# A linear-attention and token-MLP kernel: a fixed order of work, mix in token order, and stores of whole tiles

## The chip, the cores and the metric

The kernel runs on one core of one Trainium2 chip. The metric is the device time of one execution in microseconds (us), as the median of several executions. A profile is one execution; its span is about 2 us shorter than its time.

PE is TensorE's matmul side and PEld its weight loads. DVE is VectorE, ACT is ScalarE, POOL is GpSimd, and SP issues transfers. A copy or activation that brings a product from PSUM to SBUF is called an eviction.

## The reference

There are 8 batches, 8 heads, 576 tokens and 64 elements per head, in fp32. This is the reference without its set-up:

```
q_p = concat(relu(q) * cos, relu(q) * sin)       # cos and sin of the token's position
k_p = concat(relu(k) * cos, relu(k) * sin)
kv  = einsum('bhsf,bhsd->bhfd', k_p, v);  z = sum of k_p over tokens
x   = (q_p kv) / (q_p z + 1e-6)                  # then heads joined: 8 x 576 x 512
wq, wk = x @ w_q, x @ w_k                        # 512 -> 64
W      = wq wk^T / 8                             # token by token, per batch
mixed  = W x
out    = relu(mixed) @ w_out                     # 8 x 576 x 512
```

The kernel never makes W: it forms wk'x (64 x 512), then mixed = wq (wk'x).

## The kernel before

A load of one head puts nine successive tokens of that head in one partition: partition d (0 to 63 for one head, 64 to 127 for the next) holds tokens 9d to 9d+8. The kernel calls the place within the nine "c". One load brings four heads, and the table numbers these groups from 0 to 15 ("heads" in some of the texts below). Everything after that runs in **slot order**, c*64 + d, while the output in memory is in **token order**, 9*d + c. The kernel before keeps slot order to the end and lets its stores do the change, with 64 rows each:

```
    def mx(b, st, eng):                      # mixed, transposed: two 128 x 288 halves
        ...
        for r in range(2):
            nc.tensor.matmul(mx_ps[:, r, 0:hs],
                kxs[b][64 * r:64 * r + 64, dmc * P:(dmc + 1) * P],
                wqTs[b][64 * r:64 * r + 64, nh, :], start=True, stop=True)
        c0 = (b % 2) * S + nh * hs
        dst = mix_sb.rearrange("p (r i) n -> p r i n", r=2)[:, :, i, c0:c0 + hs]
        nc.scalar.activation(dst, mx_ps[:, :, 0:hs], AF.Relu, scale=scale_moe)   # dense in and out
        ...

    def wout(bp, rt0, n, engs):              # output tiles of 128 slots
        ...
                nc.tensor.matmul(o_ps[:, r, :], mixs[bp][:, dmc, rt * P:(rt + 1) * P],
                    wo_sb[:, dmc, :], start=(dmc == 0), stop=(dmc == NDM - 1))
        ...
            for hi in range(2):              # two stores of 64 rows, every 9th row of the output
                bloc, j0 = divmod(P * (rt0 + r) + 64 * hi, S)
                dst = dataclasses.replace(
                    out, offset=out.offset + (2 * bp + bloc) * S * DM + (j0 // 64) * DM,
                    ap=[[C9 * DM, 64], [1, DM]])
                nc.sync.dma_start(dst, o_sb[hi * 64:hi * 64 + 64, r, :])
```

The other parts that change: x is transposed by 10 matmuls of 128 rows per half batch. wq and wk are separate products, wk with 20 matmuls of 64 columns per batch. wk'x is 5 matmuls of 512 columns. All products of the token MLP share two PSUM buffers. The order comes from one loop over pairs of heads that mixes in the MLP of earlier batches.

Of the kernel before, what the change touches and what calls it, by code (L numbers as in the profile page):

```python
# [16 lines left out]
I32 = mybir.dt.int32  # L17
AF = mybir.ActivationFunctionType
ALU = mybir.AluOpType
FMAX = 3.4028234e38  # L20
EPS_HI = 9.9837780e-07


@with_exitstack
def kernel(
# [21 lines left out]

    NB = 2 * B
# [4 lines left out]
    inp = ctx.enter_context(tc.tile_pool(name="inp", bufs=4))  # L53
    prep = ctx.enter_context(tc.tile_pool(name="prep", bufs=2))
    small = ctx.enter_context(tc.tile_pool(name="small", bufs=3))
    xpool = ctx.enter_context(tc.tile_pool(name="xpool", bufs=3))
    moe = ctx.enter_context(tc.tile_pool(name="moe", bufs=2))
    mixpool = ctx.enter_context(tc.tile_pool(name="mixpool", bufs=2))
    outpool = ctx.enter_context(tc.tile_pool(name="outpool", bufs=3))
# [3 lines left out]
    def m2_tile(dtype, name):  # L63
        return psum.tile([P, 2, 512 if dtype is FP32 else 1024], dtype,
                         name=name, tag="m2", bufs=2)

    srcs = {}
    for nm, src in (("k", k), ("q", q), ("v", v)):
        srcs[nm] = [src[b].flatten().rearrange("(pr p e) -> p pr e", pr=NPAIR, p=P)
                    for b in range(B)]  # L70
    raw = {}

    def load(H, nsplit=1, names=("k", "q", "v")):
        b, h0 = divmod(2 * H, NPAIR)
        step = 2 // nsplit
        for nm in names:
            raw[nm, H] = inp.tile([P, 2, HC], FP32, name=f"{nm}f")
        for sp in range(nsplit):
            for nm in names:
                lo = sp * step  # L80
                nc.sync.dma_start(raw[nm, H][:, lo:lo + step, :],
                                  srcs[nm][b][:, h0 + lo:h0 + lo + step, :])

    load(0, nsplit=2)

    warm = consts.tile([P, 512], BF16)
    nc.vector.memset(warm, 1.0)
    warm_ps = m2_tile(FP32, "warm_ps")

    def warm_up(n):  # L90
        for _ in range(n):
            nc.tensor.matmul(warm_ps[:, 0, :], warm[:, 0:P], warm,
                             start=True, stop=True)

    warm_up(14)

    wq_f = consts.tile([P, NDM, DH], FP32)
    wk_f = consts.tile([P, NDM, DH], FP32)
    wo_f = consts.tile([P, NDM, DM], FP32)

    coef = math.pi / 2.0 / S
    ki = consts.tile([P, C9, 2], I32)
    qi = consts.tile([P, C9, D], I32)
    for hh in range(2):
        ph = slice(64 * hh, 64 * hh + 64)
        nc.gpsimd.iota(ki[ph, :, 0], pattern=[[-1, C9]], base=S, channel_multiplier=-C9)
        nc.gpsimd.iota(ki[ph, :, 1], pattern=[[1, C9]], base=0, channel_multiplier=C9)
    nc.gpsimd.iota(qi[0:64], pattern=[[-1, C9], [-C9, D]], base=S, channel_multiplier=0)
    nc.gpsimd.iota(qi[64:128], pattern=[[1, C9], [C9, D]], base=0, channel_multiplier=0)
    cossin = consts.tile([P, C9, 2, D], BF16)  # L110
    cst = consts.tile([P, C9, D], BF16)
    nc.scalar.activation(cossin, ki.unsqueeze(3).to_broadcast([P, C9, 2, D]),
                         AF.Sin, bias=0.0, scale=coef)
    nc.scalar.activation(cst, qi, AF.Sin, bias=0.0, scale=coef)

    ident = consts.tile([P, P], BF16)
    make_identity(nc, ident)

    ones_t = consts.tile([P, P], BF16)
    nc.gpsimd.memset(ones_t, 1.0)  # L120
    eps_t = consts.tile([P, SC], BF16)
    nc.gpsimd.memset(eps_t, 0.0)
    nc.gpsimd.memset(eps_t[0:1, :], EPS_HI)
    nc.gpsimd.memset(eps_t[32:33, :], 1.0e-6 - EPS_HI)

    v_bufs, qpt_bufs, xT_bufs = [], [], []
    for i in range(3):
        vb = consts.tile([P, 2, C9, D + 2], BF16, name=f"v_buf{i}")
        nc.gpsimd.memset(vb[:, :, :, D:D + 2], 1.0)
        v_bufs.append(vb)  # L130
    for i in range(3):
        qb = consts.tile([P, 2, SLOTS, D], BF16, name=f"qpt_buf{i}")
        nc.gpsimd.memset(qb[:, :, 0, :], 0.0)
        qpt_bufs.append(qb)
    for i in range(2):
        xb = consts.tile([P, NDM, SLOTS * D], BF16, name=f"xT_buf{i}")
        nc.gpsimd.memset(xb[:, :, 0:D], 0.0)
        xT_bufs.append(xb)

    wqq_sb = consts.tile([P, NDM, 2, DH], BF16)  # L140
    wk_sb = consts.tile([P, NDM, DH], BF16)
    wo_sb = consts.tile([P, NDM, DM], BF16)

    def load_w():
        nc.sync.dma_start(wq_f, moe_w_q.rearrange("(c p) j -> p c j", p=P))
        nc.sync.dma_start(wk_f, moe_w_k.rearrange("(c p) j -> p c j", p=P))
        nc.sync.dma_start(wo_f, moe_w_out.rearrange("(c p) n -> p c n", p=P))

    def cast_w(part):
        if part == 0:  # L150
            nc.scalar.copy(wqq_sb, wq_f.unsqueeze(2).to_broadcast([P, NDM, 2, DH]))
            nc.scalar.copy(wk_sb, wk_f)
        else:
            nc.scalar.copy(wo_sb[:, 2 * part - 2:2 * part, :],
                           wo_f[:, 2 * part - 2:2 * part, :])

    kp, qd, rks = {}, {}, {}

    def relu_k(H, lo, hi, eng):
        if lo == 0:  # L160
            rks[H] = prep.tile([P, 2, C9, D], BF16, name="rk")
        o = rks[H][:, lo:hi].rearrange("p r c d -> p r (c d)")
        if eng is nc.scalar:
            nc.scalar.activation(o, raw["k", H][:, lo:hi, :], AF.Relu)  # L164
        else:
            eng.tensor_scalar(o, raw["k", H][:, lo:hi, :], FMAX, 0.0,
                              op0=ALU.min, op1=ALU.max)

    def mul_k(H, lo, hi):
        if lo == 0:  # L170
            kp[H] = prep.tile([P, 2, C9, 2, D], BF16, name="kp")
        n = hi - lo
        nc.vector.tensor_mul(  # L173
            kp[H][:, lo:hi],
            rks[H][:, lo:hi].unsqueeze(3).to_broadcast([P, n, C9, 2, D]),
            cossin.unsqueeze(1).to_broadcast([P, n, C9, 2, D]))

    def cast_v(H, lo, hi, eng):
        src = raw["v", H][:, lo:hi, :].rearrange("p r (c d) -> p r c d", c=C9)
        dst = v_bufs[H % 3][:, lo:hi, :, 0:D]  # L180
        if eng is nc.scalar:
            nc.scalar.copy(dst, src)
        else:
            eng.tensor_scalar(dst, src, 1.0, 1.0, op0=ALU.mult, op1=ALU.mult)  # L184

    def dup_q(H, lo, hi, eng):
        if lo == 0:
            qd[H] = prep.tile([P, 2, C9, 2, D], BF16, name="qd")
        n = hi - lo
        dst = qd[H][:, lo:hi].rearrange("p r c w d -> p (r c) w d")  # L190
        src = raw["q", H][:, lo:hi, :].rearrange(
            "p r (c d) -> p (r c) d", c=C9).unsqueeze(2).to_broadcast(
                [P, n * C9, 2, D])
        if eng is nc.scalar:
            nc.scalar.activation(dst, src, AF.Relu)
        else:
            eng.tensor_scalar(dst, src, FMAX, 0.0, op0=ALU.min, op1=ALU.max)  # L197

    xs, kvs, xTs, wkjs, wqTs, kxs, mixs = {}, {}, {}, {}, {}, {}, {}

    def qk_pe(g):
        H, i = divmod(g, 2)
        qk_ps = psum.tile([P, 2, 2048], mybir.dt.uint8, name="qk_ps", bufs=1)
        qt = qk_ps[:, :, 0:2 * HC].bitcast(BF16)
        kvp = qk_ps[:, :, 2 * HC:2 * HC + 4 * (D + 1)].bitcast(FP32)
        for c in range(C9):
            for hh in range(2):
                p0 = hh * 64
                nc.tensor.matmul(  # L209
                    kvp[:, hh, :], kp[H][p0:p0 + 64, i, c, :, :],  # L210
                    v_bufs[H % 3][p0:p0 + 64, i, c, 0:D + 1],
                    start=(c == 0), stop=(c == C9 - 1))
        for c in range(C9):
            for hh in range(2):
                p0 = hh * 64
                nc.tensor.transpose(  # L216
                    qt[:, hh, c * D:(c + 1) * D],
                    qd[H][p0:p0 + 64, i, c, :, :],
                    ident[p0:p0 + 64, p0:p0 + 64])
        kv_sb = small.tile([P, 2, D + 1], BF16, name="kv_sb")  # L220
        nc.vector.tensor_copy(kv_sb, kvp)  # L221
        kvs[g] = kv_sb
        nc.vector.tensor_mul(  # L223
            qpt_bufs[g % 3][:, :, 1:SLOTS, :],
            qt.rearrange("f h (c d) -> f h c d", c=C9),
            cst.unsqueeze(1).to_broadcast([P, 2, C9, D]))
# [226 lines left out]
```

## Time and profile before

| | before |
|---|---|
| time, median of 3 | 151.56 us (150.58 to 152.74) |
| span of the profile | 149.6 us |
| PE, DVE, ACT, POOL busy | 115.7, 90.6, 88.1, 56.8 us |
| granted TensorE clock | mostly about half from 10 to 30 us, nearly always full after that |

The prediction shows the rows of busy time and of transfers. Three more lines are needed later. The first two are from the groups of instructions: line, engine, operation, output and input, shapes, count, then busy time in us and mean ns of one, then the idle time before them and what ended it. The third is the main transfer queue: packets, MB, and its share of 16 engines' span.

```profile
L316 ACT ACTIVATE mix_sb<-mx_ps 128x576 bf16<-128x576 f32 x29 | 17.5, 655 | 4.7 <-PE mx_ps L309 4.7
L309 PE MATMUL mx_ps<-wqT,kx 64*128 64x288 bf16 x64 | 8.0, 285 | 7.0 <-ACT xT_buf L260 3.9
...
q1 hardware_dynamic: 20448, 39.07, 81.2%
```

The mix evictions are a small group, 17.5 us of ACT at **655 ns** each. The queue's share is 81.2% of 149.6 = 122 us.

### The profile page before, as it was taken

What the parts mean: (1) busy time and instruction counts of PE and PEld (TensorE: products, weight loads), DVE (VectorE), ACT (ScalarE), POOL (GpSimd) and SP (SyncE); (2) the same over time, 40 slices, a digit from 0 to 9 for tenths busy, and PEclk for the clock granted to TensorE, in tenths of its full rate; (3) what the DMA queues carried; (4) which work ended last, traced back from release to release, by engine and by line L of the source; (5) the groups of instructions that cost most, each with busy time, mean ns of one, the idle gap of its engine ahead of it and who ended that gap; (6) DMA issues with size and microseconds to landing.
All of it is one profiled execution on the core that took longest, in us unless ns stands there. A gap on an engine that the chain in (4) does not pass through costs nothing. (4 is left out here: it accounts for less than half of the span.)

```text
span 149.6 us, 4978 instructions
## 1 busy us (share of the span) xinstructions
PE 115.7 (77%) x2155; PEld 77.5 (52%) x2182; DVE 90.6 (61%) x156; ACT 88.1 (59%) x114; POOL 56.8 (38%) x56
## 2 busy tenths in 40 slices
PE   6924663969889988998898987888989896894910
PEld 2214553856567657654765665557656664461400
DVE  1278363979777685947596957375959563325110
ACT  8230076467977787668768757687784566243220
POOL 7638248683561808160817164408170000000000
PEclk9985576589999999999999999999999999999996
DMA  5999999999988999996999998999921811566195
GB/s 163 307 397 338 390 391 391 391 390 390 391 279 182 332 302 323 328 379 148 296 326 343 318 400 278 314 296 307 329 81 42 184 31 24 116 143 142 24 203 124
DMA packets 20469, 39.38 MB, mean 263 GB/s; under 512 B 3040, under 2 KB 3040, under 8 KB 20448
## 3 DMA queue, kind: packets, MB, share of 16 engines
q1 hardware_dynamic: 20448, 39.07, 81.2%
q8 instruction: 17, 0.28, 0.7%
q14 instruction: 4, 0.03, 0.1%
HBM read 29.62 MB, written 9.44 MB: 261 GB/s over the span
## 5 line engine op out<-in xcount | busy, mean ns | idle before, releaser
L197 POOL TENSOR_SCALAR qd<-qf 128x2304 bf16<-128x2304 f32 (+1 forms) x17 | 35.6, 2092 | 52.1 <-PE qk_ps L216 30.6
L327 PE MATMUL o_ps<-wo_sb,mix_sb 128*128 128x512 bf16 x124 | 33.6, 379 | 3.6 <-ACT mix_sb L316 1.8
L164 ACT ACTIVATE rk<-kf 128x1152 bf16<-128x1152 f32 (+1 forms) x17 | 18.9, 1111 | 18.4 <-DMA kf<-in_k_dram 9.2
L260 ACT COPY o_sb<-o_ps 128x512 f32<-128x512 f32 (+1 forms) x24 | 18.4, 765 | 17.9 <-PE o_ps L327 8.3
L242 DVE TENSOR_TENSOR x_sb<-num_ps,rec 128x640 bf16<-128x640 f32 x32 | 26.4, 825 | 1.1
L221 DVE CAST kv_sb<-qk_ps 128x130 bf16<-128x130 f32 x32 | 9.4, 293 | 26.7 <-PE qk_ps L216 26.4
L209 PE MATMUL qk_ps<-v_buf,kp 64*128 64x65 bf16 x576 | 15.8, 199 | 11.0 <-POOL v_buf L184 7.2
L223 DVE TENSOR_TENSOR qpt_buf<-qk_ps,cst 128x1152 bf16<-128x1152 bf16 x32 | 23.9, 748 | 0.0
L173 DVE TENSOR_TENSOR kp<-rk,cossin 128x2304 bf16<-128x2304 bf16 (+1 forms) x17 | 22.2, 1305 | 1.6 <-ACT rk L164 1.6
L327 PEld LDWEIGHTS <-mix_sb 128*128 128x128 bf16 x144 | 13.3, 97 | 15.2 <-issue 3.1
L209 PEld LDWEIGHTS <-kp 64*128 64x128 bf16 x576 | 11.9, 99 | 17.2 <-issue 8.7
L316 ACT ACTIVATE mix_sb<-mx_ps 128x576 bf16<-128x576 f32 x29 | 17.5, 655 | 4.7 <-PE mx_ps L309 4.7
L260 ACT COPY xT_buf<-xT_ps 128x1152 bf16<-128x1152 bf16 x15 | 16.8, 1119 | 4.8 <-PE xT_ps L252 4.8
L184 POOL TENSOR_SCALAR v_buf<-vf 128x1152 bf16<-128x1152 f32 x15 | 17.3, 1151 | 1.2
L236 PE MATMUL num_ps<-kv_sb,qpt_buf 128*128 128x65 bf16 x320 | 17.4, 202 | 0.0
L236 PEld LDWEIGHTS <-qpt_buf 128*128 128x128 bf16 x320 | 13.4, 102 | 3.6 <-issue 1.7
L216 PE MATMUL qk_ps<-ident,qd 64*128 64x64 bf16 x576 | 14.8, 197 | 0.0
L309 PE MATMUL mx_ps<-wqT,kx 64*128 64x288 bf16 x64 | 8.0, 285 | 7.0 <-ACT xT_buf L260 3.9
L252 PE MATMUL xT_ps<-ident,x_sb 128*128 128x128 bf16 x160 | 12.2, 227 | 0.2 <-ACT mix_sb L316 0.2
L216 PEld LDWEIGHTS <-qd 64*128 64x128 bf16 x576 | 11.8, 100 | 0.0
L252 PEld LDWEIGHTS <-x_sb 128*128 128x128 bf16 x160 | 10.4, 102 | 1.9 <-issue 0.2
L239 PE MATMUL num_ps<-eps_t,ones_t 128*128 128x5 bf16 x64 | 11.2, 174 | 0.0
(44 smaller groups left out, 97.9 us busy)
## 6 DMA issues: line engine op xcount, KB each, us to landing
out_dram<-o_sb SPq DMA_DIRECT2D x72, 128.0 KB, 3.3
kf<-in_k_dram SPq DMA_DIRECT2D x15, 576.0 KB, 6.7
qf<-in_q_dram SPq DMA_DIRECT2D x15, 576.0 KB, 7.7
vf<-in_v_dram SPq DMA_DIRECT2D x15, 576.0 KB, 8.5
wo_f<-in_moe_w_out_dram SPq DMA_DIRECT2D x1, 1024.0 KB, 9.9
kf<-in_k_dram SPq DMA_DIRECT2D x2, 288.0 KB, 4.0
qf<-in_q_dram SPq DMA_DIRECT2D x2, 288.0 KB, 4.3
vf<-in_v_dram SPq DMA_DIRECT2D x2, 288.0 KB, 5.3
```

The lines of the kernel that those rows point to most:

```text
L164: nc.scalar.activation(o, raw["k", H][:, lo:hi, :], AF.Relu)
L173: nc.vector.tensor_mul(kp[H][:, lo:hi], rks[H][:, lo:hi].unsqueeze(3).to_broadcast([P, n, C9, 2, D]), cossin.unsqueeze(1).to_broadcast([P, ...
L197: eng.tensor_scalar(dst, src, FMAX, 0.0, op0=ALU.min, op1=ALU.max)
L209: nc.tensor.matmul(kvp[:, hh, :], kp[H][p0:p0 + 64, i, c, :, :], v_bufs[H % 3][p0:p0 + 64, i, c, 0:D + 1], start=(c == 0), stop=(c == C9 - 1))
L216: nc.tensor.transpose(qt[:, hh, c * D:(c + 1) * D], qd[H][p0:p0 + 64, i, c, :, :], ident[p0:p0 + 64, p0:p0 + 64])
L223: nc.vector.tensor_mul(qpt_bufs[g % 3][:, :, 1:SLOTS, :], qt.rearrange("f h (c d) -> f h c d", c=C9), cst.unsqueeze(1).to_broadcast([P, 2, ...
L236: nc.tensor.matmul(nv[:, hh, u, :], qpt_bufs[g % 3][:, hh, 2 * u:2 * u + 2, :], kvs[g][:, hh, :], start=(u == 0), stop=False)
L242: nc.vector.tensor_tensor(xs[b][:, :, 2 * pr:2 * pr + 2, :].rearrange("p u h d -> p h u d"), nv[:, :, :, 0:D], rec.to_broadcast([P, 2, SC, ...
L252: nc.tensor.transpose(xT_ps[:, i, u * P:(u + 1) * P], xs[b][:, u, 2 * hp:2 * hp + 2, :], ident)
L260: nc.scalar.copy(dst, src)
L316: nc.scalar.activation(dst, mx_ps[:, :, 0:hs], AF.Relu, scale=scale_moe)
L327: nc.tensor.matmul(o_ps[:, r, :], mixs[bp][:, dmc, rt * P:(rt + 1) * P], wo_sb[:, dmc, :], start=(dmc == 0), stop=(dmc == NDM - 1))
```

## The change

The intent is to drop the loop's order for a table that places each piece of work, on its engine and in its PSUM bank, and to save work on the way. TensorE gets cheaper transposes, wq and wk come from one product, and wk'x runs in pairs of 64-column tiles. Mix is written in token order, so a store is 128 partitions with whole rows next to each other. The core of the diff:

```diff
-    inp = ctx.enter_context(tc.tile_pool(name="inp", bufs=4))
+N_RAW, N_RK, N_KP, N_QD, N_VB, N_QPT, N_KV = 5, 2, 3, 3, 3, 4, 4
+N_XS, N_XT, N_WQK, N_WKJ, N_KX, N_MIX, N_OSB = 3, 2, 2, 2, 2, 2, 5
+ORDER = """
+LD.k.0.0@Y LD.k.0.1@Y LD.q.1.0@Y LD.k.1.0@Y LD.v.1.0@Y LD.q.0.1@Y LD.v.0.1@Y LD.q.0.0@Y
+... (55 lines in all: piece @ engine and, for TensorE, PSUM bank)
+"""
+    banks = psum.tile([P, 8, 2048], U8, name="banks")
 ...
-                nc.tensor.transpose(xT_ps[:, i, u * P:(u + 1) * P],
-                    xs[b][:, u, 2 * hp:2 * hp + 2, :], ident)
+                for r in range(2):
+                    p0 = 64 * r
+                    T.transpose(xv[:, r, i, u, :],
+                                xs[b % N_XS][p0:p0 + 64, u, 2 * hp:2 * hp + 2, :],
+                                ident[p0:p0 + 64, p0:p0 + 64])
 ...
-                nc.tensor.matmul(wk_ps[:, 0, u * DH:(u + 1) * DH], ...)       # 20 per batch
+                T.matmul(w[:, nh, :], wqk_sb[:, dmc, :], ...)                  # wq and wk at once
+            T.transpose(t[:, u * DH:(u + 1) * DH], wqk[b % N_WQK][64:128, u * P:(u + 1) * P], ...)
 ...
-            nc.tensor.matmul(kx_ps[:, 0, :], wkjs[b][:, u, :, :], xs[b][:, u, :, :], ...)
+            for r in range(2):
+                T.matmul(o[64 * r:64 * r + 64, :], wkj[b % N_WKJ][:, u, :],
+                         xs[b % N_XS][:, u, 4 * r:4 * r + 4, :], ...)
 ...
-        dst = mix_sb.rearrange("p (r i) n -> p r i n", r=2)[:, :, i, c0:c0 + hs]
+        c0, c1 = ((0, 5), (5, 9))[nh]
+        src = bank2(at["MX", b, j], 0, 4 * n, FP32).rearrange(
+            "p r (c d) -> p r c d", d=D)
+        dst = mix[b // 2 % N_MIX].rearrange("p (r i) n -> p r i n", r=2)[
+            :, :, i, o:o + S].rearrange("p r (d c) -> p r c d", c=C9)[:, :, c0:c1, :]
 ...
+            cols = mix[b // 2 % N_MIX][:, dmc, base:base + step * P].rearrange(
+                "p (n s) -> p s n", s=step)[:, r, :]
 ...
-                nc.sync.dma_start(dst, o_sb[hi * 64:hi * 64 + 64, r, :])
+        eng.dma_start(out_rows[r0:r0 + step * P, :].rearrange("(p s) n -> p (s n)", s=step),
+            osb[n % N_OSB][:, 0:step, :].rearrange("p s n -> p (s n)"))
```

## The prediction

> **What bounds the kernel now.** I read the page first, then busy time by stretches, then the waits, then the timeline of one steady period. From the page (part 1's PE row; then granted clock, DMA share and GB/s over 40 slices of 3.74 us):
>
> ```profile
> PE 115.7 (77%) x2155; PEld 77.5 (52%) x2182; DVE 90.6 (61%) x156; ACT 88.1 (59%) x114; POOL 56.8 (38%) x56
> ...
> PEclk9985576589999999999999999999999999999996
> DMA  5999999999988999996999998999921811566195
> GB/s 163 307 397 338 390 391 391 391 390 390 391 279 182 332 302 323 328 379 148 296 326 343 318 400 278 314 296 307 329 81 42 184 31 24 116 143 142 24 203 124
> ```
>
> No engine is full over the span. The first 42 us run at 390 GB/s: there loads are the limit, and TensorE, short of work, falls to half clock (10 to 30 us). After that come stretches, in which one holds neither loads nor full engines:
>
> ```profile
> 60.00:80.00 20.00, 18.13 (x340) 11.92 (x345) 15.01 (x26) 14.06 (x19) 8.54 (x5) 1.00 0.92 299
> ...
> 110.00:120.00 10.00, 9.07 (x202) 6.23 (x203) 6.77 (x13) 6.01 (x9) 1.15 (x1) 1.00 0.48 106
> 120.00:130.00 10.00, 8.14 (x110) 5.12 (x110) 4.40 (x9) 5.72 (x8) 0.00 (x0) 1.00 0.25 56
> 130.00:140.00 10.00, 7.52 (x57) 4.01 (x59) 3.49 (x5) 3.33 (x7) 0.00 (x0) 1.00 0.48 107
> ```
>
> Columns: stretch, length, busy PE, PEld, DVE, ACT, POOL, granted clock, DMA share, GB/s. From 60 to 80 us PE is 91% busy and DMA 92%. In the last three rows there are hardly any loads: DMA at share 0.48 moves 106 GB/s, that is 106/0.48 = 221 GB/s per full share, where the loads made 390 at a share of about 1.06 (the stretches of 10 to 30 us), 369. So **a stored byte costs DMA 1.7 times a loaded one**. 29.62/0.369 + 9.44/0.221 = 80 + 43 = 123 us of DMA share, and 81.9% of 149.6 us is 122.5: it adds up.
>
> The steady period (one batch) is 62.00 to 77.10 us on the timeline, 15.1 us. Its pieces, by start to start (a PE end is modelled, so busy time overstates):
>
> ```profile
> 68.92 0.82 DVE L242 TENSOR_TENSOR x_sb<-num_ps,rec 128x640 bf16<-128x640 f32 x1
> 69.66 1.35 DVE L173 TENSOR_TENSOR kp<-rk,cossin 128x2304 bf16<-128x2304 bf16 x1
> ...
> 71.06 0.30 DVE L221 CAST kv_sb<-qk_ps 128x130 bf16<-128x130 f32 x1
> 71.27 0.75 DVE L223 TENSOR_TENSOR qpt_buf<-qk_ps,cst 128x1152 bf16<-128x1152 bf16 x1
> 71.33 0.72 PE L252 MATMUL xT_ps<-ident,x_sb 128*128 128x128 bf16 x10
> 73.25 0.74 PE L268 MATMUL wk_ps<-wk_sb,xT_buf 128*128 128x64 bf16 x20 [0.34 <-ACT xT_buf L260]
> 74.95 1.24 PE L293 MATMUL kx_ps<-x_sb,wkj 128*128 128x512 bf16 x4
> ```
>
> PE per batch: 4 k/v and q-transpose blocks of 0.65 (2.6), 4 numerators of 0.35 (1.4), 2 xT of 0.55 (1.1), wk 0.67, wk'x 1.08, wq 1.07, mix 0.72, 4.5 output tiles of 0.86 (3.9): 12.5 us, so 2.6 of 15.1 are waits. DVE per pair of heads: 0.21 + 0.67 + 0.25 + 0.74 + half of 1.40 = 2.57, four make 10.3 us. DMA per batch: 3.54 MB at 390 plus 1.18 MB at 221 x 1.06 = 9.1 + 5.0 = 14.1 us. **The steady part is thus bound by PE's order and its waits, with DMA only 1.0 us behind**; from 110 us on it is a serial tail. The waits say the same, the others wait for PE:
>
> ```profile
> POOL qd L197 <- PE qk_ps L216: 30.6, 8, 5.8
> DVE kv_sb L221 <- PE qk_ps L216: 26.4, 16, 2.6
> ```
>
> **What the Trainium skill says.** "SBUF — State Buffer", section "Door 1: The DMA port swizzle": partitions 0..63 reach 8 of 16 ports, with an asymptote of half the rate. The 64-row stores here at 221 against 369 agree in direction; the 128-row ones should then cost what loads cost. The same page, "Who interferes with whom": a DVE instruction with two SBUF inputs and a GpSimd one that reads SBUF exclude each other, the second waits. The trace agrees: these two rows are 0.43 and 0.85 us longer than their usual 1.35 and 2.11, and each began while the other engine's was running.
>
> ```profile
> 28.09 1.78 DVE L173 TENSOR_TENSOR kp<-rk,cossin 128x2304 bf16<-128x2304 bf16 x1
> 11.83 2.96 POOL L197 TENSOR_SCALAR qd<-qf 128x2304 bf16<-128x2304 f32 x1 [2.58 <-DMA qf<-in_q_dram]
> ```
>
> "TensorEngine Tiling (Array Packing)", "Tiling Modes": 64-row and 64-column tiles run in parallel, but a change of mode drains. For rows the trace agrees (18 of the 64-row matmuls start within 0.29 us, 16 ns each, where 64 columns at full clock alone would be 29 by the page "TensorE: Matmul & The Clock Gate", "Back-to-back issue gap": N/2.4 + 2.5); for column tiles no run here shows it yet.
>
> **The change part by part** (counts from the table of the changed kernel, durations from above).
> *PE.* xT becomes 20 transposes of 64 rows: 20 x 16 ns = 0.32 for 0.55, twice, -0.46. The 20 wk matmuls go (-0.67), 5 small transposes come (+0.13). wk'x is 10 matmuls of 256 columns in pairs: 0.54 for 1.08 if the pair runs together, no gain if not. Sum: 12.5 - 1.5 = 11.0 us per batch.
> *DMA.* Stores of 128 rows and 4 KB: if they cost what loads do, 39.07 MB/390 = 100 us in all for 116 at before's rates, 12.1 us per batch. Input rings go from 4 to 5 deep and stores are placed where their data is ready, so SP should not block loads. All inputs and the stores ahead of the last load are 33 MB: that load lands at 33/0.39 + 2.5 = 87 us at best.
> *ACT and POOL.* ACT gives 9 of the k relus to POOL and some evictions to DVE and takes 8 v casts: about 78 us. POOL about 59 + 4. Neither binds.
> *DVE.* The base stays 32 x 2.57 = 82 us. From ACT it gets 7 output evictions, 4 xT, 4 mix, 4 smaller, one copy and one relu: 21 pieces of about 0.65 less 0.08 overlap, 13 to 14 us. Sum **96 us: DVE becomes the fullest engine**, 11 to 14 us in each batch's part of the table (PE 8 to 12, DMA 11 to 13 there).
>
> *The path.* (a) Start: head pairs 3 and 2 come first. Their loads are 2.36 MB; in the kernel before that many bytes had landed at about 10.3 us; a v cast of 1.16 follows; first matmul at 11.5 to 12, with DVE having done 2.7 us of its 96. (b) From there to the last wq/wk product, DVE has 88.8 us in the table. If it were never idle the middle would take 88.8. I add two terms: collisions with POOL, which is busy over half of this time now while before it mostly started behind PE (3 collisions in 15): 16 products x 0.3 us = 5 us; and 6% idle from an order that waits for evictions and, at the start, from a half-clock PE: (88.8 + 5)/0.94 = 99.8. Here the 6% is my choice. (c) Tail from the last wq/wk product: PE has 11.9 us in the table; the chain of product, eviction, transpose, eviction, wk'x, eviction, mix, two evictions, five output tiles, eviction is about 11.5 to 12.2. Then a store: about 3 us where before needed 6.4 after its last eviction (143.15 to 149.6) as stores were queued. 15.3. Sum 12 + 99.8 + 15.3 = 127.1 for the span; time was span + 2.0 before: **129**; with no collisions and no idle it would be 118. I put the point between, nearer the first, as a fixed table is likely to have been fitted to such durations: **127.5**.
>
> **Rivals.** (1) *DMA takes over*: if mixed stores still cost 221, the stores before the last load add 3.4 MB x (1/0.234 - 1/0.39) = 6 us, last load at 93; behind it about 5 us to the last x, still not later than DVE (12 + 88.8). It would cost 0 to 4 us. For it: shares of 0.92 already now. Against: the port argument. (2) *Fixed order, PE stalls*: PE is in order too; wherever the table's guess of a landing time is wrong, every engine waits in turn. Eight PSUM banks instead of a fixed pair per use speak against; the idle would then be 12 to 15%, and the time 134 to 138. (3) *POOL and DVE lock each other* more: all 16 products wait 0.85 us (a mean rest of a POOL piece), 13 us instead of 5: 136. (4) *Nothing is gained since DMA was near its bound anyway*: against it is the 42 us tail after 107 us with DMA at 0.2 to 0.5, of which the change takes about half by starting the later batches' work earlier.
>
> **Range and chances.** Low: 118 plus a little, 120. High: rivals 2 or 3 at full size, 136. Faster by over 2% needs less than 148.5, which takes 20 us of idle on top: 0.96. Same 0.025, slower 0.015.
>
> **What would show it.** Right: DVE busy near 100 us and over 75% of the span; the k product's mean above 1.4 us; first k/v matmul near 12 us; stores alone at over 300 GB/s per share; loads finished before 95 us; wk'x half as long start to start; under 4 us from last eviction to end. Wrong: a largest wait of DVE on PE still over 20 us; a DMA share of 0.95 or more up to the last load with DVE waiting for inputs; strided output weights making the output tile slower than 0.86 us; PE at half clock beyond 35 us.

## The result

The changed kernel takes **185.49 us** (median of 4, 184.87 to 187.64), and the kernel before 151.07 in the same rounds. Ratios here are the mean time of one kernel's fast runs over that of the other's of the same rounds, so not quite the ratio of the medians. This one is 1.235, with a 95% interval of 1.224 to 1.246. The change made the kernel 23% slower, where the prediction said 127.5 and gave "slower" a chance of 0.015.

The page of the changed kernel: busy time by engine, then granted clock, DMA share and GB/s over 40 slices of 4.65 us, the main transfer queue, and the chain of work that ended last, by engine and by line.

```profile
PE 130.0 (70%) x2262; PEld 82.6 (44%) x2262; DVE 105.1 (57%) x177; ACT 132.6 (71%) x111; POOL 66.5 (36%) x60
...
PEclk9955855996579579965859786995598559985599
DMA  5999999999993086028999918100052022021245
GB/s 167 326 402 392 378 361 390 388 390 390 391 389 131 0 261 240 4 99 304 374 350 379 301 49 303 60 4 0 0 231 111 28 90 99 18 113 56 113 174 221
...
q1 hardware_dynamic: 17904, 39.06, 57.7%
...
PE 40%; ACT 33%; issue 11%; DVE 8%; DMA 5%; SPq 1%; ACTq 0%; DVEq 0%
ACT mix L385 29%; PE banks L402 13%; PE banks L243 6%; PE banks L275 6%; DMA vf<-in_v_dram 5%; PE banks L252 5%; PE banks L326 3%; DVE mix L387 3%; PE banks L371 3%; PE banks L354 2%; DVE kp L215 2%; PE banks L309 2%; DVE qpt L262 2%; ACT xT L170 1%; SPq L191 1%
```

ACT has gone from 88.1 to 132.6 us and is now the engine with the largest share. The granted clock falls to half again and again in the whole span: its mean is 0.761, where it is 0.925 in experiment 1, which has the same table and short evictions. The queue's share did what was hoped: 57.7% of 185.9 = 107 us, where it had 122. The groups say where ACT's time went:

```profile
L385 ACT ACTIVATE mix<-banks 128x640 bf16<-128x640 f32 (+1 forms) x28 | 75.0, 2811 | 8.7 <-PE banks L371 8.7
...
L371 PE MATMUL banks<-wqk,kx 64*128 64x320 bf16 (+1 forms) x32 | 10.3, 345 | 12.7 <-ACT mix L385 12.6
...
L387 DVE TENSOR_SCALAR mix<-banks 128x640 bf16<-128x640 f32 (+1 forms) x4 | 10.7, 2769 | 3.7 <-PE banks L371 3.7
```

One mix eviction costs **2811 ns where it cost 655**, on DVE 2769. They move as much as before: 640 and 512 elements by turns, for 576. So 28 of them fill 75.0 us of ACT. The last line of the page's chain has these evictions as 29% of the span on ACT and 3% on DVE, so they are on the path, and a piece of the timeline shows how (start, length, engine, what; in brackets the idle time before and what ended it):

```profile
57.32 3.35 ACT L385 ACTIVATE mix<-banks 128x640 bf16<-128x640 f32 x1
60.72 0.42 PE L371 MATMUL banks<-wqk,kx 64*128 64x320 bf16 x1 [3.84 <-ACT mix L385]
61.20 3.01 ACT L385 ACTIVATE mix<-banks 128x640 bf16<-128x640 f32 x1 [0.54 <-PE banks L371]
62.71 0.29 DVE L172 CAST kvs<-banks 128x130 bf16<-128x130 f32 x1 [4.02 <-PE banks L252]
64.26 0.68 PE L243 MATMUL banks<-vb,kp 64*128 64x65 bf16 x18 [1.59 <-ACT mix L385]
```

PE waits 3.84 us for an eviction to give back its banks. DVE waits 4.02 us for PE. Then the next eviction holds PE again.

### The profile page after: what moved, and what is told of

The parts are those of the page before. It is cut to its first block, busy times and chain, and to the rows that moved or that the text cites. A ratio compares the mean times of both kernels' runs of the same rounds, so it can differ in the third digit from the quotient of the medians.

```text
span 185.9 us, 5159 instructions
## 1 busy us (share of the span) xinstructions
PE 130.0 (70%) x2262; PEld 82.6 (44%) x2262; DVE 105.1 (57%) x177; ACT 132.6 (71%) x111; POOL 66.5 (36%) x60
## 3 DMA queue, kind: packets, MB, share of 16 engines
q1 hardware_dynamic: 17904, 39.06, 57.7%
## 4 chain that ended last, share of the span: by engine, by line
PE 40%; ACT 33%; issue 11%; DVE 8%; DMA 5%; SPq 1%; ACTq 0%; DVEq 0%
ACT mix L385 29%; PE banks L402 13%; PE banks L243 6%; PE banks L275 6%; DMA vf<-in_v_dram 5%; PE banks L252 5%; PE banks L326 3%; DVE mix L387 3%; PE banks L371 3%; PE banks L354 2%; DVE kp L215 2%; PE banks L309 2%; DVE qpt L262 2%; ACT xT L170 1%; SPq L191 1%
## 5 line engine op out<-in xcount | busy, mean ns | idle before, releaser
L385 ACT ACTIVATE mix<-banks 128x640 bf16<-128x640 f32 (+1 forms) x28 | 75.0, 2811 | 8.7 <-PE banks L371 8.7
L402 PE MATMUL banks<-wo_sb,mix 128*128 128x512 bf16 x144 | 45.3, 458 | 5.2 <-ACT mix L385 3.8
L262 DVE TENSOR_TENSOR qpt<-banks,cst 128x1152 bf16<-128x1152 bf16 x32 | 23.6, 749 | 16.9 <-PE banks L252 13.6
L243 PE MATMUL banks<-vb,kp 64*128 64x65 bf16 x576 | 18.9, 217 | 16.6 <-ACT mix L385 6.9
L275 PE MATMUL banks<-kvs,qpt 128*128 128x65 bf16 x320 | 18.7, 216 | 10.7 <-ACT mix L385 8.9
L292 DVE TENSOR_TENSOR xs<-banks,rec 128x640 bf16<-128x640 f32 x32 | 25.3, 807 | 0.2
L275 PEld LDWEIGHTS <-qpt 128*128 128x128 bf16 x320 | 17.3, 113 | 16.6 <-issue 12.8
L170 ACT COPY osb<-banks 128x512 f32<-128x512 f32 x29 | 19.2, 674 | 6.7 <-PE banks L402 6.6
L170 ACT COPY xT<-banks 128x1280 bf16<-128x1280 bf16 x12 | 15.2, 1263 | 6.1 <-PE banks L309 6.0
L180 POOL TENSOR_SCALAR rk<-kf 128x1152 bf16<-128x1152 f32 (+1 forms) x11 | 12.9, 1170 | 16.7 <-DVE kp L215 15.3
L252 PE MATMUL banks<-ident,qd 64*128 64x64 bf16 x576 | 18.2, 215 | 0.0
L387 DVE TENSOR_SCALAR mix<-banks 128x640 bf16<-128x640 f32 (+1 forms) x4 | 10.7, 2769 | 3.7 <-PE banks L371 3.7
```

What stands on the lines that cost most here:

```text
L170: A.copy(dst, src)
L180: eng.tensor_scalar(dst, src, FMAX, 0.0, op0=ALU.min, op1=ALU.max)
L243: T.matmul(kvp[:, hh, :], kp[H % N_KP][p0:p0 + 64, i, c, :, :], vb[H % N_VB][p0:p0 + 64, i, c, 0:D + 1], start=(c == 0), stop=(c == C9 - 1))
L252: T.transpose(qt[:, hh, c * D:(c + 1) * D], src, ident[p0:p0 + 64, p0:p0 + 64])
L262: eng.tensor_mul(qpt[g % N_QPT][:, :, 1:SLOTS, :], qk_views(at["QK", g])[0].rearrange("f h (c d) -> f h c d", c=C9), cst.unsqueeze(1).to_b ...
L275: T.matmul(nv[:, hh, u, :], qpt[g % N_QPT][:, hh, 2 * u:2 * u + 2, :], kvs[g % N_KV][:, hh, :], start=(u == 0), stop=(u == SC - 1 and not ...
```

## The experiments

The first question was what makes the eviction slow. The changed write is the suspect: its last dimension steps through mix by 9 elements, 18 bytes, where before it was dense. Rival A: it is the eviction's other new features (larger pieces, reading from banks shared by all). Rival B: the table itself starves the kernel, and slow evictions only show it. The second question, once that was known, was why the mended kernel is still 10 us above the prediction.

### 1. Only the write made dense (a wrong result)

```diff
-            :, :, i, o:o + S].rearrange("p r (d c) -> p r c d", c=C9)[:, :, c0:c1, :]
+            :, :, i, o:o + S].rearrange("p r (c d) -> p r c d", c=C9)[:, :, c0:c1, :]
```

The rows then come out in slot order (relative error 0.498), and all else is as in the changed kernel.

> The changed kernel with one edit: the mix evictions write side by side in slot order instead of every 18 bytes, so output rows are in the wrong places on purpose; table, counts and sizes are as they were. Theory A (the stride of 18 bytes makes each of the 32 mix evictions 2.8 us in place of about 0.7): evictions 0.6 to 0.75 us, ACT busy falls from 132.6 by 28 x 2.1 = 59 to about 74 us, time 120 to 135 us. Rival B (the fixed order itself stalls, and the long evictions are a symptom of waiting on something): evictions stay above 2 us or the time stays above 165 us.

Measured: 137.85 us (137.08 to 139.06), ratio to before 0.914 (0.905 to 0.924). The same groups, with the shapes kept apart:

```profile
L385 ACT ACTIVATE mix<-banks 128x640 bf16<-128x640 f32 x14 | 9.9, 706 | 12.0 <-PE banks L371 8.5 <-PE banks L402 3.5
L385 ACT ACTIVATE mix<-banks 128x512 bf16<-128x512 f32 x14 | 8.2, 597 | 8.8 <-PE banks L371 4.5 <-PE banks L402 4.3
```

This one line of addressing is worth 47.6 us. ACT's evictions lost 75.0 - 18.1 = 56.9 us and DVE's 10.7 - 3.0 = 7.7. The time gained is three quarters of that. PE's busy time fell too, from 130.0 to 105.8 us, as the clock stayed up. Rivals A and B fall: size, banks and table are unchanged. The same table also gives a kernel faster than the one before.

### 2. Token order read from PSUM (correct)

The change of order moves to the other side. The product covers 32 of the 64 partitions' tokens, so that one eviction holds 288 whole successive tokens. The eviction reads PSUM with a step and writes densely.

```diff
-            w = (wqk[...][0:64, D + c0 * D:D + c1 * D] if r == 0
-                 else wq2[...][64:128, c0 * D:c1 * D])
+            w = (wqk[...][0:64, D:D + S] if r == 0 else wq2[...][64:128, :]).rearrange(
+                     "p (c d) -> p c d", c=C9)[:, :, d0:d1]     # d0, d1 = 0, 32 or 32, 64
 ...
-            "p r (c d) -> p r c d", d=D)
+            "p r (c d) -> p r d c", c=C9)                        # source: step of 32 in PSUM
-            :, :, i, o:o + S].rearrange("p r (d c) -> p r c d", c=C9)[:, :, c0:c1, :]
+            :, :, i, o:o + n].rearrange("p r (d c) -> p r d c", c=C9)   # dense
```

> Token order kept and result right: mix products are cut by the 32-token halves instead of by slots, so an eviction reads PSUM with a stride of 128 bytes and writes 288 neighbours densely. Theory A1 (only strided writes into SBUF are slow): evictions about 0.7 us, time as e1. Theory A2 (strided reads of PSUM cost the same): evictions 2.3 to 3 us, time 180 to 190 us.

Measured: **137.91 us** (137.42 to 139.6), ratio 0.911 (0.900 to 0.922), correct.

```profile
L385 ACT ACTIVATE mix<-banks 128x576 bf16<-128x576 f32 x28 | 17.9, 652 | 20.0 <-PE banks L372 12.2 <-PE banks L402 7.7
```

An eviction that reads PSUM with a step of 128 bytes costs 652 ns, as much as the dense one of the kernel before. So token order itself costs nothing; the side on which it is made decides.

### 3. Token order read by TensorE (correct)

Here the matmul's moving operand is read in token order, and the eviction is dense on both sides.

```diff
-            ... else wq2[...][64:128, c0 * D:c1 * D])
+            ... else wq2[...][64:128, :]).rearrange("p (c d) -> p d c", c=C9)[:, d0:d1, :]
```

> Token order kept and result right: the permutation is done by TensorE, whose moving operand of the mix product is read with a stride of 128 bytes; evictions are dense on both sides. Theory A with a free strided moving read: time as e1 (120 to 135 us). If the moving read is slowed by 4 like the writes, the 64 mix matmuls go from about 125 to 500 ns, pairs side by side, 12 us more TensorE work: 125 to 147 us. Rival B: above 165 us.

Measured: 141.25 us (140.29 to 142.2), ratio 0.936 (0.926 to 0.946).

```profile
L372 PE MATMUL banks<-wqk,kx 64*128 64x288 bf16 x32 | 19.6, 644 | 1.8 <-ACT mix L384 1.7
...
127.59 0.66 PE L372 MATMUL banks<-wqk,kx 64*128 64x288 bf16 x1
128.07 0.66 PE L372 MATMUL banks<-wqk,kx 64*128 64x288 bf16 x1
```

One mix product takes 644 ns where it takes 296 in experiment 2, and the kernel is 3.3 us slower than experiment 2 (141.25 against a mean of 137.95 of the fast runs). The mean of one hides the true price, because successive products overlap. Start to start, two of them lie 0.48 us apart in the two lines of the timeline above, and 0.12 us in experiment 2 (125.88 and 126.00 us), both at full granted clock. So TensorE pays for the step too, by about the same factor of four as ACT, on less work: 32 pairs times 0.36 us are 11.5 us (an estimate from these starts), of which 3.3 reached the time.

### 4. The stepped write put into the kernel before (a wrong result)

```diff
-        dst = mix_sb.rearrange("p (r i) n -> p r i n", r=2)[:, :, i, c0:c0 + hs]
+        dst = mix_sb.rearrange("p (r i) n -> p r i n", r=2)[:, :, i, c0:c0 + hs].rearrange(
+            "p r (d c) -> p r c d", c=C9)            # every 9th place of the half's 288
+        src = mx_ps[:, :, 0:hs].rearrange("p r (c d) -> p r c d", c=C9)
-            nc.scalar.activation(dst, mx_ps[:, :, 0:hs], AF.Relu, scale=scale_moe)
+            nc.scalar.activation(dst, src, AF.Relu, scale=scale_moe)
```

> The kernel before with only the write of its mix evictions changed to a step of 9 elements (rows wrong on purpose). Theory A: 29 evictions on ACT and 3 on DVE go from 0.66 to about 2.6 us, ACT busy from 88 to about 145 us, time 180 to 205 us. Rival B (the write is harmless, the table is the cause): 150 to 156 us.

Measured: 206.49 us (203.37 to 210.49). Two of its four runs, the profiled one among them, were slow, so the 2867 ns below come from a slow run; the two fast ones took 205.85 and 203.37, ratio 1.356 (1.334 to 1.378).

```profile
L318 ACT ACTIVATE mix_sb<-mx_ps 128x576 bf16<-128x576 f32 x29 | 76.6, 2867 | 5.5 <-PE mx_ps L309 5.5
```

The write alone brings the evictions of the kernel before to 2867 ns, as in the changed one, and costs it 53 us. With experiment 1 this is the cause from both ends: taken away, it gives 47.6 us back; put in, it takes 53.

### 5. The cost of a step, measured by itself

Experiment 2 was followed, after its last product, by copies of 256 elements per partition with various steps, three of each (one look; 198.45 us with these copies).

```diff
+    for _ in range(3):
+        A.copy(flatA[:, 0:256*s].rearrange("p (n s) -> p n s", s=s)[:, :, 0], flatB[:, 0:256])
+    ...  # s = 1 to 16; the same for DVE, for fp32, for PSUM and SBUF reads, for TensorE's operands
```

> Measures the disputed cost by itself: the kernel of e2, and after its end 256-element copies from PSUM to SBUF on ACT and DVE, each line with one step between written elements (bf16 steps 1 to 16, fp32 steps 1 to 8), then strided reads of PSUM and of SBUF, then matmuls with a strided moving operand and strided weights. Theory A: on both engines the write costs about 1 cycle per element while at least two elements fall into the same 16 bytes, and about 4 times as much once each falls into a line of its own: the jump lies between bf16 steps 4 and 9 and between fp32 steps 2 and 4; PSUM reads show none of it (e2 did not slow down). For the moving operand e3 says 644 against 296 ns for 288 columns at 128 bytes: about twice per column. A rival to the line theory, a cost that grows smoothly with the step, would show no jump.

ACT writing bf16 from PSUM with steps of 1 and 8 elements (the table has the others), then reading PSUM in runs with a step of 32, then TensorE's moving operand with steps of 4 and 8:

```profile
L474 ACT CAST mix<-banks 128x256 bf16<-128x256 f32 x3 | 1.1, 374 | 0.1
L488 ACT CAST mix<-banks 128x256 bf16<-128x256 f32 x3 | 3.9, 1289 | 0.1
...
L516 ACT CAST mix<-banks 128x256 bf16<-128x256 f32 x3 | 1.1, 372 | 0.1
...
L582 PE MATMUL banks<-mix,wo_sb 128*128 128x256 bf16 x8 | 2.0, 407 | 0.0
L584 PE MATMUL banks<-mix,wo_sb 128*128 128x256 bf16 x8 | 3.8, 630 | 0.0
```

| step of a bf16 write | 1 | 2 | 3 | 4 | 6 | 8 | 9 | 16 |
|---|---|---|---|---|---|---|---|---|
| ACT, ns for 256 | 374 | 443 | 584 | 726 | 1007 | 1289 | 1281 | 1279 |
| DVE, ns for 256 | 422 | 443 | 583 | 726 | 1007 | 1287 | 1278 | 1277 |

I had expected a jump; for bf16 it is a smooth rise. From step 2 to step 8 each step adds about 141 ns, that is 141/32 = 4.4 ns for each further 16 bytes that the 256 elements span, and above 16 bytes it stays flat. At a step of 9 this is about 160 + 4.4 ns an element. For 640 elements that makes 2976 ns, where the changed kernel's evictions of that shape took 3061, and for 512 it makes 2413 for 2562: an estimate from this table, 3 and 6% short. It is the same on both engines, so handing evictions to DVE does not help. PSUM reads cost the same at every step tried (372 to 389 ns on ACT, 419 to 424 on DVE). fp32 writes follow another curve: 500 ns dense, 385 at step 2, 495 at step 3, 607 at step 4.

The same run has two more readings. Stepped reads of SBUF (bf16 to fp32) do cost something: ACT took 404, 424, 669 and 662 ns at steps 1, 4, 9 and 16, DVE 295, 295, 400 and 403. So it is the read of PSUM that was free, not a stepped read as such. TensorE's moving operand of 256 columns came 0.21 to 0.23 us apart, start to start, at steps 1, 2 and 4 (granted clock about half), and 0.45 to 0.46 us at steps 8, 9 and 16, whether the granted clock was 1.00 (step 8) or 0.50 (9 and 16). So the "about twice" that I had expected holds at half clock; at full clock it is the factor of four of experiment 3.

### 6. Only the stores, in the kernel before (correct)

Token order read from PSUM as in experiment 2, and stores of 128 rows, in the order and with the other operations of the kernel before.

```diff
-                nc.sync.dma_start(dst, o_sb[hi * 64:hi * 64 + 64, r, :])
+        nc.sync.dma_start(out.rearrange("b s n -> (b s) n")[r0:r0 + n * P, :].rearrange(
+                "(r p) n -> p r n", p=P), o_sb[:, 0:n, :])
```

> One part alone in the kernel before, result right: token order by strided PSUM reads and whole-tile 128-row stores, its own order kept. If a stored byte then costs DMA what a loaded one does, share times span falls from 122 us to about 106 us; the tail after the last eviction falls from 6.4 to about 3 us. Theory C (the gain of e2 over the kernel before, 14 us, is mostly stores): 138 to 143 us. Theory D (it is mostly the table, the extra banks and fewer TensorE cycles; stores give only the end): 145 to 149 us.

Measured: 148.56 us (148.11 to 148.91), ratio 0.981 (0.972 to 0.989).

```profile
q1 hardware_dynamic: 19680, 39.06, 74.3%
```

The queue's share falls from 122 us to 74.3% of 146.9 = 109 us, but the time by only 2%. After the last eviction the kernel needs 4.3 us, for 6.4 before; I had expected about 3. So the stores' saving is real and mostly hidden. By subtraction, some 11 us of the gain of experiment 2 come from the other parts (table, banks, fewer TensorE cycles), taken together. Two things changed in a store at once, 128 partitions for 64 and neighbouring rows for every ninth; no run separates them.

### 7. Stores issued by ACT (correct)

In experiment 2 SP waited 59 us in all for output evictions before it could issue a store, with the loads queued behind it. Here stores go to ACT's queue.

```diff
-ST.0.1@Y ...
+ST.0.1@A ...        # all 22 stores; nothing else moved
```

> e2 with the 22 stores issued by ACT instead of SP, nothing else changed. In e2 loads stand on SP behind stores that wait for evictions (SP waits 59 us there, and DMA falls to 108 and 7 GB/s in two slices near 66 us). If this head-of-line wait delays the products, the hole vanishes, loads end before 90 us and the time falls by 3 to 7 us to 131 to 135. If DVE and TensorE have slack for it: 136 to 139. If ACT loses more by issuing (22 x 0.4 us and waits for DVE's evictions in its order): above 139.

Measured: 137.83 us (135.94 to 138.53; two of four runs slow), ratio 0.902 (0.890 to 0.913).

```profile
DMA  4899999999999999999999999604018340341484
GB/s 146 280 391 401 393 394 332 361 371 395 389 390 392 391 392 390 391 407 394 392 392 411 405 417 370 271 16 157 7 77 349 121 162 31 128 190 42 192 342 165
```

Loads now run at a full queue without a hole until 85 us. The last load is issued at 82.6 us where it was 90.7. The time hardly moves: the intervals of experiments 2 and 7 overlap. Blocked loads were not the missing 10 us.

### 8 to 13. What holds the mended kernel at 137 us

All but experiment 8 start from experiment 7, whose fast runs have a mean of 136.6 us; experiment 8 starts from experiment 2. Each relieves one suspect.

Experiment 8 gives POOL's k relus to ACT (correct):

```diff
-RK.3.0@G ...
+RK.3.0@A ...        # all 11 that POOL had
```

> e2 with the 11 k relus that the table gives to POOL given to ACT, same places in the order. In e2 the k products on DVE take 1.70 us in the mean against 1.35, and two of them near 62 to 67 us take 3.02 and 2.31 us, while POOL runs. If the exclusion of DVE and POOL costs what the means say (14 x 0.35 = 5 us of DVE, the fullest engine), the mean falls to about 1.5 and the time by 2 to 4 us. If ACT, now with 13 us more at fixed places, makes others wait instead: 137 to 142.

Measured: 138.98 us, ratio 0.917 (0.909 to 0.925). No gain.

Experiment 9 leaves out POOL's relu, cast and copy from group 4 on (wrong):

```diff
+            if where == "G" and name in ("RK", "CV", "DQ") and args[0] >= 4:
+                continue
```

> The kernel with dense evictions and the stores on ACT (137.8 us), with POOL's relu, v cast and q copy left out from head 4 on; the rings keep old rows, so the result is wrong on purpose. It bounds from above what POOL costs the others. If POOL and DVE shutting each other out is a large part of the 10 us between 127.5 and 137.8: kp products fall from 1.84 us to about 1.35, DVE busy from 99.6 to about 94, and the time to 131 to 134. If the first 80 us are set by the transfers (the queue was full there) and the last 50 by PE, the kp products fall all the same, and the time stays within 2 us of 137.8.

Measured: 136.95 us, ratio 0.910 (0.906 to 0.915).

```profile
L215 DVE TENSOR_TENSOR kp<-rk,cossin 128x2304 bf16<-128x2304 bf16 (+1 forms) x18 | 22.8, 1264 | 4.9 <-ACT rk L178 4.8
```

The k product falls from 1653 to 1264 ns, so POOL did cost DVE 7.0 us in all. The fast runs have a mean of 136.6, the same as with POOL. This does not mean that the collisions were off the path. In experiment 7 the chain that ended last is 47% PE, 25% DVE (the k products alone 11%) and 6% DMA. Without POOL's work it is:

```profile
DMA 39%; PE 33%; SPq 8%; ACT 7%; issue 6%; DVE 2%; ACTq 1%; POOL 1%; DVEq 0%; POOLq 0%
```

So the path moved from DVE to the loads, which stood right behind.

Experiment 10 gives eight small copies from DVE to ACT (correct):

```diff
-EX.4@V  EX.10@V  EX.11@V  EO.0.3@V  EO.1.4@V  EO.2.1@V  EWK.4@V  EW.5@V
+EX.4@A  EX.10@A  EX.11@A  EO.0.3@A  EO.1.4@A  EO.2.1@A  EWK.4@A  EW.5@A
```

> Correct. The same kernel with eight small copies of the middle (three x copies, three output tiles, two copies behind the wq/wk product) given from DVE to ACT, whose 77 us leave it room; DVE loses some 5 us of work. If DVE's own work sets the middle: 133 to 135 us. If transfers and PE set it: 136.5 to 138.5.

Measured: 138.78 us, ratio 0.918 (0.909 to 0.927); the profiled run was slow. DVE has 6 us less to do (93.6 for 99.6), and nothing is gained. But ACT, which got the copies, goes from 7% to 11% of the chain, so this run can't tell slack in DVE from a gain that ACT took away.

Experiment 11 leaves out half of the contraction of the output products of batches 3 to 7 (wrong), 9.9 us of PE's work:

```diff
-        for dmc in range(NDM):
+        for dmc in range(NDM if b < 3 else 2):
```

> The same kernel with half of the contraction of the output products left out for batches 3 to 7 (wrong on purpose): 23 tiles x 0.43 us = 9.9 us of PE's work gone, nearly all of it after 80 us, where PE was 90 to 95% busy. If PE sets the second half and the tail: 128 to 131 us. If DVE, transfers or the fixed order set it, only the tail's last few tiles count: 134 to 137.

Measured: 132.39 us (131.96 to 133.56), ratio 0.881 (0.875 to 0.887). Its four runs are all fast, with a mean of 132.6: **4.0 us less, the largest effect of these six** and the only one whose interval does not overlap that of experiment 7, though the time stays above the 128 to 131 that a pure PE bound should have given. The profiled runs (135.4 and 130.5 us) show where it was gained. From the last wq/wk product to the end 19.4 us became 16.8; 11 of the 23 halved tiles lie there. From the first k/v product to the last wq/wk product 103.4 became 102.2, though the other 12 tiles lie there; and 1.1 us came before the first k/v product, where the edit changes nothing.

Experiment 12 leaves out the v loads of groups 5 to 15 (wrong), 16.6 us of transfer:

```diff
+            if name == "LD" and args[0] == "v" and args[1] >= 5:
+                continue
```

> The kernel with dense evictions and the stores on ACT (137.8 us), with the v loads of heads 5 to 15 left out (wrong on purpose): 11 x 0.59 MB = 6.5 MB, 16.6 us at the 392 GB/s of its first 82 us. If the transfers alone hold the first 82 us: 130 us or less. If DVE's work stands right behind them there, as much as taking POOL away stood behind: 135.5 to 137.5, with the DMA share no longer full.

Measured: 135.63 us, ratio 0.896 (0.889 to 0.902): about 1 us, with intervals that overlap. The full queue of the first 85 us hides behind something else.

Experiment 13 does 9 and 12 at once (wrong).

> The same with POOL's relu, v cast and q copy left out from head 4 on as well (wrong on purpose). If transfers and the POOL/DVE collisions hold the first 82 us side by side, taking both away gives what neither gave alone: 128 to 133 us. If PE or the fixed order holds it: within 2 us of the kernel without POOL's work, 135 to 138.

Measured: 135.41 us; two of four runs slow, the profiled one among them; the fast ones 133.23 and 134.54, ratio 0.885 (0.874 to 0.895). This is 2.7 us below experiment 7, on two fast runs, and the intervals overlap. It lies above the 128 to 133 of one theory and, with its fast runs, below the 135 to 138 of the other, so it decides for neither alone. Busy time by stretches (columns as in the prediction), first of experiment 7, then of experiment 13:

```profile
40.00:80.00 40.00, 32.63 (x869) 22.65 (x871) 35.19 (x56) 25.91 (x38) 28.26 (x19) 1.00 1.05 397
80.00:100.00 20.00, 17.92 (x384) 11.97 (x376) 17.31 (x33) 13.03 (x21) 10.67 (x8) 1.00 0.46 178
100.00:116.00 16.00, 15.28 (x345) 9.38 (x342) 13.48 (x26) 10.25 (x16) 3.12 (x4) 1.00 0.41 163
```

```profile
40.00:80.00 40.00, 33.88 (x811) 23.31 (x811) 30.95 (x57) 26.27 (x38) 2.74 (x3) 0.91 0.80 291
80.00:100.00 20.00, 19.86 (x448) 13.63 (x448) 18.32 (x36) 14.50 (x23) 0.78 (x1) 1.00 0.17 68
100.00:116.00 16.00, 15.28 (x341) 9.65 (x340) 12.54 (x24) 10.24 (x15) 0.67 (x1) 1.00 0.42 167
```

With transfers and POOL out of the way, PE is 99% busy from 80 to 100 us and 95% from 100 to 116. DVE's share of the chain that ended last falls from 25% to 13%, and PE's rises from 47% to 61%. From 80 us on PE is the fullest engine, in experiment 7 too (90 and 96%). That its work is worth time is shown for the tail (experiment 11), not for 80 to 116 us. Before that PE (82%), DVE (88%) and the queue (full) stand close together, and relieving one or two of them gave 0 to 3 us.

### The results side by side

Times are medians of all runs, ratios are of fast runs; experiments 8 to 10, 12 and 13 are above.

| kernel | time, us | ratio to before |
|---|---|---|
| before | 151.07 | 1 |
| the change | 185.49 | 1.235 |
| 1: write dense (wrong order) | 137.85 | 0.914 |
| **2: order read from PSUM** | **137.91** | **0.911** |
| 3: order read by TensorE | 141.25 | 0.936 |
| 4: before with stepped write (wrong) | 206.49 | 1.356 |
| 6: before with whole-tile stores | 148.56 | 0.981 |
| **7: as 2, stores from ACT** | **137.83** | **0.902** |
| 11: as 7, half of late output products (wrong) | 132.39 | 0.881 |

Experiments 2 and 7 are correct and beat both kernels.

## Why the prediction was wrong

**The step that failed is one sentence: "ACT gives 9 of the k relus to POOL and some evictions to DVE and takes 8 v casts: about 78 us … Neither binds."** The 78 us hold the 28 mix evictions at the 0.66 us that they took before, although the diff shows that their write no longer is dense. They took 2.81 us. 78 + 28 x (2.81 - 0.66) = 138 us, and ACT was busy for 132.6. The list of risks named the stepped read of the output weights, which did no harm, and not the stepped write. Row tiles and bytes were priced from the trace, and the column tiles were marked as not yet seen; the access pattern of an unchanged operation was not looked at.

The miss was readable in advance. The Trainium skill, "SBUF — State Buffer", in its note on cachelines under "Door 1: The DMA port swizzle", says that an access that crosses to a new 16-byte line pays a penalty and that 8 bf16 is as far as one can step for free. A step of 9 is past that, and experiments 1 and 4 agree with the direction. I used that section for the ports alone. No page gives the size for ACT or DVE, 4.4 ns an element here.

**A second step failed, by its size: the 6% of idle time in part (b) of the path.** With the write mended, the time is still 10 us above 127.5. Experiments 2 and 7 let the other steps be checked one by one:

- **Start (a)**: first k/v matmul predicted at 11.5 to 12 us; it came at 12.09 and 12.62. Right to within 0.6 us.
- **Transfers**: stores at the price of loads. The queue's share fell from 122 to 107 us, and the prediction's 39.07 MB at loads' 0.369 MB per us of full share make 106. Right in size; that the number of partitions is the reason is not shown (experiment 6).
- **PE's savings**: 20 transposes of 64 rows take 0.30 us start to start for 0.32 predicted. wk'x in pairs takes 0.67 us where it took 1.08: the pair runs together, short of the 0.54. PE's busy time fell from 115.7 to 103.9 us in experiment 7.
- **DVE's work and collisions**: DVE was busy for 97.9 and 99.6 us for 96 + 5. (The sum has a slip: 21 pieces of 0.65 less 0.08 are 12 us, not 13 to 14.) The mean of a full k product is 1.70 and 1.84 us, above 1.4 as foretold. The collisions are there, but experiment 9 shows that taking them away gains nothing, as the loads take their place on the path.
- **Middle (b)**: 99.8 us predicted; 106.6 and 103.4 measured. The sum took DVE as the bound, with 88.8 + 5 us of work and 6% idle. The work was sized well: in this stretch DVE is busy for 89.0 and 90.7 us. But it is idle for 16.5 and 12.2% of it. The waits listed for it in this stretch are all for PE's products, 17.1 us in experiment 2 and 12.3 in experiment 7 (there 6.0 for the k/v products and q transposes, 3.7 for the numerators). PE, whose work was cut, is still busier over the span (103.9 us) than DVE (99.6), so DVE was not the one engine to sum.
- **Tail (c)**: 15.3 us predicted; 18.5 and 19.4 measured. The store at the end fits (2.9 us after the last eviction, for about 3), the part before it does not. In experiment 2 ACT's mix evictions wait 7.7 us in all, over the whole run, for output products of PE.

**The rivals.** Rival 2 ("fixed order, PE stalls", with 12 to 15% idle and 134 to 138 us) has the size of what is left, 137.8, and nearly the idle share, 12 to 16%. That PE's output products are worth time in the tail is shown (experiment 11). That the order of the table causes the rest is only argued: no run had another order. Rival 1 (transfers) alone gives 0 to 1 us (experiments 7 and 12), rival 3 (POOL and DVE) alone nothing (experiment 9), both together 2.7 us, not clear of the noise (experiment 13). No rival held the cause of the miss.

What stays open: how much of the 10 us between 127.5 and 137.8 another order would give back, and what holds the stretch from 80 us to the last wq/wk product, where 12 halved output tiles gained about 1 us.

## What to carry to other kernels

When a diff changes only the access pattern of an operation, price that operation anew: look at the byte step of its last dimension on each side, and measure it with a few copies at the end of a kernel. If data must change its order on the way from PSUM to SBUF, step through PSUM on the read and write SBUF densely; here that cost nothing, the stepped write cost four times the eviction, and TensorE's stepped read four times the product, start to start. When several engines and the queue stand within 20% of each other, relieving one of them buys little, and the idle share of the fullest engine is not a small term: here it was 12 to 16%, where 6% was assumed.

## What the Trainium skill lacked or had wrong

- "SBUF — State Buffer", "Door 1: The DMA port swizzle", note on cachelines: it gives 8 bf16 as the step that is free. For bf16 writes by ACT and DVE nothing above 1 was free: 443 ns at step 2, 726 at 4, 1289 at 8, for 374 (ACT) and 422 (DVE) at 1, and flat from 16 bytes on. The growth is smooth, 4.4 ns per 16 bytes. Reads of SBUF at step 4 were free or nearly so (DVE 295 ns for 295, ACT 424 for 404), and at step 9 they were not (400 and 669); step 8 was not read by these two. The page gives no size for the penalty.
- The same note does not tell bf16 from fp32 in cost: an fp32 write that steps by 16 bytes took 607 ns for 256 elements (500 when dense), the bf16 one 1289. Why is open.
- No page says what a stepped PSUM read by ACT or DVE costs: it cost nothing (372 to 389 ns on ACT, 419 to 424 on DVE, at all steps tried). The note's warning on PSUM patterns is for matmuls, and no run here compares a stepped write of a matmul with a dense one.
- No page has the cost of a stepped moving operand: 0.48 us start to start for 0.12 on 288 columns with a step of 128 bytes, at full granted clock; in the products at the end of experiment 5, 0.45 to 0.46 us for 256 columns from 16 bytes on, at half and at full clock alike, and no clear difference from dense up to 8 bytes.
- "TensorEngine Tiling (Array Packing)", "Tiling Modes", has different tiles run in parallel. Products in two 64-column tiles did so in part: ten of 256 columns took 0.67 us, where half of the old 1.08 would be 0.54.
